# Turning keys and queries over in 64x64 quadrants in an attention and ReGLU kernel

## The chip, the cores and the metric

The kernel runs on one core of a Trainium2 chip. The metric is the device time of one execution in microseconds. The core has a matrix engine (TensorE, PE in the profile) that writes to PSUM, eight banks of 128 partitions by 512 fp32 values; three engines for elementwise work and reductions (VectorE or DVE, ScalarE or ACT, GpSimd or POOL); and DMA queues, of which this kernel uses that of SyncE (SP) for nearly everything and that of GpSimd for the weights of the feed-forward part.

## The reference

Eight batches of eight heads, 576 tokens, 64 values per head. Each head sees 16 "beacon" keys and values ahead of its own 576, the beacons from every row, the others causally. The heads are put side by side to 4608 tokens of 512 values, and a ReGLU feed-forward network follows.

```python
k_all = np.concatenate([beacon_k, k], axis=2)          # 16 + 576 = 592 keys
v_all = np.concatenate([beacon_v, v], axis=2)
scores = scale * np.matmul(q, k_all.transpose(0, 1, 3, 2))
scores = np.where(causal, -1000000000.0, scores)
a = np.exp(scores - scores.max(-1, keepdims=True))
a /= a.sum(-1, keepdims=True) + 1e-09
attn = np.matmul(a, v_all)
x = attn.transpose(0, 2, 1, 3).reshape(4608, 512)
out = (np.maximum(x @ w_gate, 0.0) * (x @ w_val)) @ w_out   # 512 -> 1536 -> 512
```

## The kernel before, in words

**Attention of one batch.** Heads are handled in four pairs, one head on partitions 0 to 63 and one on 64 to 127, so that a score matmul has 64 values to contract and TensorE can run four 64x64 quadrants side by side. Batch by batch, `new_batch` (line 497) loads the keys and queries of each pair (`load_pair`, 552), the last 64 keys with the beacons and the first and last queries (`load_rest`, 610) and the values (`load_v`, 647). A load lands as fp32 in one of eight staging buffers, is cast to bf16 into one of three cast buffers (`rounded`, 508; on GpSimd from batch 1 on) and is turned over so that the 64 values of a head lie on partitions.

In batches 0 to 6 that is done by TensorE: `turned` (522) issues four matmuls of 128x128 against an identity (line 529) into one PSUM bank, and ScalarE or VectorE evicts the bank to `kT` or `qT` (copies at 467 and 469). A load brings four neighbouring tokens (1 KB) to one partition, so the eviction puts columns back in order with a strided read. In batch 7 (`TURN`) a DMA transpose does it (574); its loads bring single tokens of 256 bytes (560).

**Scores to outputs.** `quad_scores` (727) computes a causal staircase of 64-query tiles for two pairs at a time, in the 64x64 shape (line 756). `softmax` (680) works along each row: minimum of negated scores and mask in one VectorE instruction (704), exponential with row sum on ScalarE (711), reciprocal on VectorE (717), normalisation in place on GpSimd (722). From batch 3 on a step takes two to four tiles. `last` (797) does the 16 last queries of all heads with 32-column tiles (806). `finish` (815) turns the probabilities over, by DMA except in batch 0 (and the last rows of batch 1), multiplies by the values (852, 875; shape 128x64 or 128x128) and copies to `xT`.

**Feed-forward.** `ffn` (905) takes ten spans of 240 to 512 tokens: gate (913) and value (918) matmuls, ReLU on ScalarE (924), product on VectorE (929), output matmuls (944), a copy and a store. A span waits for the batches that its tokens come from.

**What sets the order.** All of this is handed as tasks to a planner (`Plan`, 174) that simulates engines, buffers and DMA with costs written by hand and emits every engine's instructions in the order of that simulation. For each choice it takes the earliest possible start, then a term `late` for TensorE, then the priority. `late` belongs to the shape of the array: a task has a `part` (0: 128x128, 1: values, 2: scores, 3: last rows), a change costs SWITCH = 0.1, a task of the present part comes first, and a task with `lazy` of n may be put off up to n us while others run. Line 236:

```python
late = -1 if part and t.part == part else NEXT if part and t.part else \
    1 if part != t.part and at < t.ready + t.lazy else 0
```

BACKLOG limits how far loads and stores are issued ahead of the modelled wire. PACE x batch is the earliest planned start of a batch's scores. LAZY = 20 is the patience of the values. HELD and BEHIND hold single loads back: a tiny memset on GpSimd (539) must run before the load, and itself waits for a weight or, through BEHIND, for the normalised halves of an earlier batch. SC_MOST, V_MOST and F_MOST (5, 3, 3) limit how many PSUM banks scores, turns and values, and the feed-forward hold. Where TensorE has nothing planned before 160 us, filler matmuls (996) are put in.

Of the kernel before, what the change touches and what calls it, by code (L numbers as in the profile page):

```python
# [18 lines left out]

BACKLOG = 4.0  # L20
RANK1 = -14.0
AHEAD = 2.0
# [10 lines left out]
SLAZY = 0.0  # L33
NEXT = -0.5
ON_PE = 2
TURN = (7,)
TURN_FIRST = 100
# [27 lines left out]
AFTER = [[0.0, 12.0]]  # L65
PACE = 38.0

# [229 lines left out]
def kernel(  # L297
# [189 lines left out]


    def heads(src, b, s0, sl):
        return src[b, :, s0:s0 + sl, :].rearrange("h s d -> s h d")  # L490
# [6 lines left out]
    def new_batch(b, prio, work):  # L497
        t = Batch()
        t.b = b
        steps = 2 * sum(len(x) for x in (STEPS2 if b > BIGSTEP else STEPS if b >= SPLIT else STEPS_AB + STEPS_CDE)) + 1  # L500
        t.kT = Hold(kT_s, 2 * (NP + 1) + steps)
# [50 lines left out]
        def load_pair(kind, p, prio):  # L552

            src, s0 = {"k": (k, 0), "q": (q, 64 - Nb)}[kind]
            st = staged()

            def fetch(_):
                if b in TURN:
# [7 lines left out]
            ld = add("DMA", (1.0, TURN_LOAD) if b in TURN else (0.5, 0.87), fetch, (held,), (st,), prio[0])  # L566
            dst = t.kT if kind == "k" else t.q
            h16, ca = rounded(dst, st, P, neg_scale if kind == "q" else 1.0, prio, ld,
                              lambda to, src: [(to, src)] if b in TURN else [(
                to.rearrange("p (j h d) -> p h j d", h=2, j=4), src.rearrange("p (h j d) -> p h j d", h=2, j=4))])  # L570
            zeros = on_zeros.get(b) if kind == "q" else None
            c0 = Nb if kind == "k" else 64
            if b in TURN:
                t.rows[kind, p] = [add("DMA", (1.22, 0.177 * 4), lambda _: nc.sync.dma_start_transpose(
                    dst.tile[:, p, c0:c0 + MAIN].rearrange("p (j n) -> p j n", j=4), h16.tile), (ca, zeros), (h16, dst), prio[0] - TURN_FIRST)]
# [7 lines left out]
            t.rows[kind, p] = [add(("ACT", "DVE"), {"ACT": c_act(512), "DVE": c_dve(512)}, evict, (tu, zeros), (ps, dst), prio[1])]  # L583

        def load_half(kind, g, half, prio):
# [24 lines left out]
        def load_rest(kind, prio):  # L610
# [21 lines left out]
            def evict(x):  # L632
                ps3 = ps.tile.rearrange("p (a n) -> p a n", a=NP)
                if kind == "k":
                    copy(x.engine, dst.tile[:, :, Nb + MAIN:], ps3[:, :, :REST])
# [26 lines left out]

        at, held = 0, None
        for what in ORDER0 if b == 0 else "KQ0011v2233vvvv":
# [15 lines left out]
    def softmax(t, parts, ph, prio, k):  # L680
# [3 lines left out]
        def view(i, lo=0):  # L684
            n, held, off = parts[i][:3]
            if len(held) == 1:
                return held[0].tile[:, off + lo:off + n]
            at = 512 * next(j for j, x in enumerate(bank) if x is held[0].tile)
            return psum[:, at + lo:at + n]

# [6 lines left out]
        for i, (n, held, _, msk, m, on, _, scored) in enumerate(parts):  # L697
            first = []
            if m < n:
                first = [add("DVE", c_max(n - m), lambda _, i=i, n=n, m=m: nc.vector.tensor_reduce(  # L700
                    out=at(7), in_=view(i)[:, :n - m], axis=AX.X, op=ALU.min), (scored,), held, prio + 0.001 * i + 0.0005 * k, 0.25)]

            def lowest(_, i=i, n=n, m=m, msk=msk):
                nc.vector.tensor_tensor_reduce(out=view(i, n - m), in0=view(i, n - m), in1=msk, scale=1.0,  # L704
                                               scalar=at(7) if m < n else 3.0e38,
                                               op0=ALU.add, op1=ALU.min, accum_out=at(i))

            lows.append(add("DVE", c_max(m), lowest, (scored, on, *first), held, prio + 0.001 * i + 0.0005 * k, 0.25))
        for i, (n, held, _, _, _, _, a, _) in enumerate(parts):
            def exp(_, i=i, n=n, a=a):  # L710
                nc.scalar.activation(ph.tile.rearrange("p a n -> p (a n)")[:, a:a + n], view(i), AF.Exp,  # L711
                                     bias=at(i), scale=-1.0, accum_out=at(4 + i))
# [14 lines left out]
    def quad_scores(t, g, step, phs, vals, prio, after):  # L727
# [23 lines left out]
        def scores(_):  # L751
            for j, lo, n, b_, off in cols:
                for i in range(2):
                    for k in ks:
                        r = slice(64 * k, 64 * k + 64)
                        nc.tensor.matmul(banks[k][b_].tile[64 * i:64 * i + 64, off:off + n],  # L756
                                         t.q.tile[r, 2 * g + i, 64 * j:64 * j + 64],
                                         t.kT.tile[r, 2 * g + i, lo:lo + n], start=True, stop=True)

# [16 lines left out]
    def quad(t, g, vals, prio, after):  # L776
# [4 lines left out]
        if PEQ(t.b, g):  # L781
            todo = list(range(NB_AB)) if ab else [i for i in range(21) if i not in (3, 7)] if t.b < SPLIT else list(range(NB))
            on_pe = [todo[i:i + 8] for i in range(0, len(todo), 8)]
        phs = [Hold(Slots([p_ab[t.b][:, 2 * g + k]]) if ab else p_s[1], max(1, len(on_pe))) for k in range(2)]
# [12 lines left out]
    def last(t, prio):  # L797
# [5 lines left out]
        def scores(_):  # L803
            for bank, a, n in ((sc[0], 0, 512), (sc[1], 512, SK - 512)):
                for pp in range(NP):
                    nc.tensor.matmul(bank.tile[32 * pp:32 * pp + 32, :n], t.q.tile[:, pp, S + Nb - TAIL:],  # L806
                                     t.kT.tile[:, pp, a:a + n], start=True, stop=True)
# [7 lines left out]
    def finish(t, p, vals, ph, pt_s, blocks, on_pe, outs, prio):  # L815

        pt = Hold(pt_s, len(vals) + max(1, len(on_pe)))
        if on_pe:
            tr = []
            for todo in on_pe:  # L820
                tp = Hold(first_ps if t.b == 0 else v_ps, 2)
                z = len(todo)
                runs = []
                for i, a in enumerate(todo):
                    if not runs or runs[-1][1] + runs[-1][2] != a:
                        runs.append([i, a, 0])
                    runs[-1][2] += 1

                def turn(_, todo=todo, tp=tp):
                    to = tp.tile.bitcast(BF16)  # L830
                    for i, a in enumerate(todo):
                        nc.tensor.transpose(to[:, i * P:(i + 1) * P], ph.tile[:, a, :], ident)  # L832

                def evict(x, runs=runs, tp=tp):
                    for i, a, n in runs:
                        copy(x.engine, pt.tile[:, a:a + n, :].rearrange("p a n -> p (a n)"), tp.tile.bitcast(BF16)[:, i * P:(i + n) * P])

                u = add("PE", 0.06 * z, turn, outs + [on_ident], (ph, tp), prio - 4)
                more = 0.07 * (len(runs) - 1)
                tr.append(add(("ACT", "DVE"), {"ACT": c_act(z * P) + more, "DVE": 0.08 + 0.0006 * z * P + more}, evict, (u,), (tp, pt), prio - 4))  # L840
        else:
# [131 lines left out]
    for b in range(B):  # L973
        batches.append(new_batch(b, {0: -20, 1: RANK1}.get(b, b * T0 - 8), b * T0 - AHEAD if b else -20))
    for b in range(B):
        for i, vals in enumerate([("AB", "CDE")] if b >= SPLIT else [("AB",), ("CDE",)]):
            for g in range(2):
                quad(batches[b], g, vals, b * T0 + (4 * g if b >= SPLIT else 4 * i + 2 * g) - (AB_FIRST if b < SPLIT and i == 0 else 0), AFTER[b][i] if b < SPLIT else PACE * (b + g / 2))
        last(batches[b], b * T0 + 8)
    for t in batches:  # L980
# [49 lines left out]
```

## Time and profile before

| | us |
|---|---|
| median of 3 runs | 402.75 |
| the runs | 399.99, 402.75, 403.11 |
| the profiled execution | 399.48 |
| span of its instructions | 397.8 |
| TensorE busy | 386.6 |
| VectorE, ScalarE, GpSimd busy | 287.6, 261.7, 234.2 |

The profile is one execution. Its views: the page (busy time of each engine, the span in 40 slices), busy time in chosen stretches, groups of instructions by line with their count, mean duration and the idle time ahead of them, who waited for whom, the timeline, and the chain of waits, which follows the work that ended last back from releaser to releaser. Matmuls overlap, so one's duration (225 ns for 128 columns) is not what it costs in a row of others; that is read from starts, or from the chain. A line number can be that of a helper: 467 and 469 are all copies on ScalarE and VectorE.

### The profile page before, as it was taken

Reading aid. Unit: us, or ns where it says so; the run is one execution under the profiler, and the core shown is the slowest. Engines: PE = TensorE matmul, PEld = TensorE weight load, DVE = VectorE, ACT = ScalarE, POOL = GpSimd, SP = SyncE. Lnnn points to the kernel's source line nnn. Section 1 sums busy time; section 2 is a strip of 40 time slices with the busy share of each in tenths; the row PEclk is TensorE's granted clock in tenths of the full one; section 3 lists DMA queues with packets and bytes.
Section 4 is the critical chain, followed back from the end, with each engine's and each line's share of the span. In section 5 each row is a group of like instructions: output and inputs, shape, how many; then the busy total and the mean of one; then the engine's idle time right before and its main releaser. Section 6 shows DMA issues by size and latency. Waiting matters only on the chain.

```text
span 397.8 us, 9897 instructions
## 1 busy us (share of the span) xinstructions
PE 386.6 (97%) x3235; PEld 203.8 (51%) x3278; DVE 287.6 (72%) x1024; ACT 261.7 (66%) x820; POOL 234.2 (59%) x454
## 2 busy tenths in 40 slices
PE   6999999999999999999999999999999999999995
PEld 4667855655454545455455445444454544444543
DVE  3999899788988697879697969687758733342432
ACT  2999699868967788668877878587737721320320
POOL 6899979849977576869669848646653520000000
PEclk9999999999999999999999999999999999999999
DMA  7999989999999799989999989798979184001102
GB/s 183 233 205 226 250 154 180 214 232 256 247 209 204 197 224 221 176 227 263 189 166 298 208 146 183 164 221 184 196 138 234 25 127 145 2 0 57 50 1 93
DMA packets 184100, 68.87 MB, mean 173 GB/s; under 512 B 158384, under 2 KB 179504, under 8 KB 184048
## 3 DMA queue, kind: packets, MB, share of 16 engines
q1 hardware_dynamic: 179216, 63.46, 73.7%
q0 software_dynamic: 4752, 4.72, 7.5%
q8 instruction: 25, 0.41, 0.5%
q14 instruction: 27, 0.22, 0.2%
q10 hardware_dynamic: 80, 0.07, 0.1%
HBM read 38.54 MB, written 9.44 MB: 121 GB/s over the span
## 4 chain that ended last, share of the span: by engine, by line
PE 88%; POOL 3%; DVE 3%; DMA 2%; issue 1%; SPq 1%; ACT 0%; POOLq 0%; ACTq 0%
PE f L918 23%; PE f L944 23%; PE f L913 22%; PE f L756 7%; PE f L852 6%; PE f L529 3%; DMA st<-in_q_dram 2%; POOL xT L722 2%; DVE f L704 2%; PE f L832 1%; PE f L996 1%; PE f L875 1%; PE f L806 1%; DVE osb L469 1%; POOL h L518 1%
## 5 line engine op out<-in xcount | busy, mean ns | idle before, releaser
L722 POOL TENSOR_SCALAR pb<-pb,small 128x448 bf16<-128x448 bf16 (+8 forms) x272 | 141.5, 539 | 70.5 <-DVE small L717 69.8
L711 ACT ACTIVATE pb<-f,small 128x320 bf16<-128x320 f32 (+8 forms) x272 | 143.9, 553 | 22.6 <-DVE small L704 17.7
L704 DVE CUSTOM_DVE_ANT_0 f<-f,mask 128x576 f32<-128x576 f32 (+8 forms) x288 | 133.7, 515 | 14.3 <-PE f L756 9.1
L918 PE MATMUL f<-xT,wv_r 128*128 128x512 bf16 (+3 forms) x467 | 107.3, 358 | 0.7
L913 PE MATMUL f<-xT,wg_r 128*128 128x512 bf16 (+3 forms) x468 | 105.4, 357 | 0.6
L929 DVE TENSOR_TENSOR hT<-g,f 128x512 bf16<-128x512 f32 (+3 forms) x120 | 75.4, 631 | 37.3 <-PE f L918 32.1
L944 PE MATMUL f<-wo_r,hT 128*128 128x512 bf16 (+3 forms) x438 | 99.6, 374 | 1.3 <-issue 0.5
L924 ACT ACTIVATE g<-f 128x512 f32<-128x512 f32 (+3 forms) x120 | 66.3, 562 | 50.9 <-PE f L913 44.2
L913 PEld LDWEIGHTS <-wg_r 128*128 128x128 bf16 x480 | 45.3, 98 | 43.7 <-issue 1.2
L918 PEld LDWEIGHTS <-wv_r 128*128 128x128 bf16 x480 | 43.4, 98 | 44.5 <-issue 5.2
L944 PEld LDWEIGHTS <-hT 128*128 128x128 bf16 (+2 forms) x456 | 42.1, 100 | 46.3 <-issue 2.1
L711 ACT ACTIVATION_READ_ACCUMULATOR pb<-f,small 128x1 f32 x272 | 60.9, 224 | 0.0
L518 POOL TENSOR_SCALAR h<-st 128x512 bf16<-128x512 f32 (+1 forms) x93 | 49.0, 541 | 11.0 <-DMA st<-in_q_dram 6.9
L469 DVE COPY osb<-f 128x512 f32<-128x512 f32 (+2 forms) x32 | 21.7, 682 | 28.1 <-PE f L944 27.7
L704 DVE DVE_READ_ACCUMULATOR2_ANT small<- 128x1 f32 x296 | 41.6, 141 | 0.0
L467 ACT CAST xT<-f 128x240 bf16<-128x240 f32 (+2 forms) x56 | 21.2, 385 | 30.7 <-PE f L852 29.5
L756 PE MATMUL f<-kT,qT 64*64 64x512 bf16 (+7 forms) x640 | 34.4, 295 | 0.1
L717 DVE RECIPROCAL small<-small 128x1 f32<-128x1 f32 (+3 forms) x136 | 20.9, 161 | 13.5 <-ACT pb L711 9.8
L529 PE MATMUL f<-ident,h 128*128 128x128 bf16 (+1 forms) x288 | 26.8, 222 | 1.6 <-POOL h L518 1.4
L529 PEld LDWEIGHTS <-h 128*128 128x128 bf16 (+1 forms) x288 | 20.0, 101 | 14.6 <-POOL h L518 4.0
L852 PE MATMUL f<-pTb,v 128*64 128x320 bf16 (+3 forms) x488 | 26.7, 253 | 0.0
L471 POOL TENSOR_SCALAR v<-st 128x512 bf16<-128x512 f32 (+1 forms) x38 | 23.2, 617 | 4.0 <-DMA st<-in_v_dram 4.0
(61 smaller groups left out, 217.5 us busy)
## 6 DMA issues: line engine op xcount, KB each, us to landing
out_dram<-osb SPq DMA_DIRECT2D x34, 256.0 KB, 2.4
st<-in_k_dram SPq DMA_DIRECT2D x28, 256.0 KB, 5.0
st<-in_q_dram SPq DMA_DIRECT2D x28, 256.0 KB, 5.1
st<-in_v_dram SPq DMA_DIRECT2D x24, 256.0 KB, 5.6
st<-in_k_dram SPq DMA_DIRECT2D x16, 128.0 KB, 4.2
st<-in_q_dram SPq DMA_DIRECT2D x16, 128.0 KB, 3.1
st<-in_v_dram SPq DMA_DIRECT2D x8, 224.0 KB, 5.2
wg_r<-in_moe_w_gate_dram POOLq DMA_DIRECT2D x3, 512.0 KB, 7.3
```

The lines of the kernel that those rows point to most:

```text
L518: (nc.gpsimd if x.engine == "POOL" else nc.vector).tensor_scalar(to, src, by, 1.0, ALU.mult, ALU.mult)
L529: nc.tensor.matmul(to, h16.tile[:rows, a * P:(a + 1) * P], ident[:rows, :rows], start=True, stop=True)
L704: nc.vector.tensor_tensor_reduce(out=view(i, n - m), in0=view(i, n - m), in1=msk, scale=1.0, scalar=at(7) if m < n else 3.0e38, op0=ALU.ad ...
L711: nc.scalar.activation(ph.tile.rearrange("p a n -> p (a n)")[:, a:a + n], view(i), AF.Exp, bias=at(i), scale=-1.0, accum_out=at(4 + i))
L722: nc.gpsimd.tensor_scalar(one, one, at(8 + i), 1.0, ALU.mult, ALU.mult)
L756: nc.tensor.matmul(banks[k][b_].tile[64 * i:64 * i + 64, off:off + n], t.q.tile[r, 2 * g + i, 64 * j:64 * j + 64], t.kT.tile[r, 2 * g + i, ...
L852: nc.tensor.matmul(ps.tile[64 * hh:64 * hh + 64, d0:d0 + w], t.v.tile[:rows, c, D * h:D * h + D], rhs(64 * hh), start=(c == 0), stop=(c == ...
L913: nc.tensor.matmul(psg.tile[:, :mt], wg_r[:, ki, nf * P:(nf + 1) * P], xT[:, ki, m0:m0 + mt], start=(ki == 0), stop=(ki == KM - 1))
L918: nc.tensor.matmul(psv.tile[:, :mt], wv_r[:, ki, nf * P:(nf + 1) * P], xT[:, ki, m0:m0 + mt], start=(ki == 0), stop=(ki == KM - 1))
L924: r = add("ACT", c_act(mt), lambda _, psg=psg, g=g: nc.scalar.activation(g.tile[:, :mt], psg.tile[:, :mt], AF.Relu), (a,), (psg, g), -1000 ...
L929: hid.append(add("DVE", c_dve(mt), lambda _, psv=psv, g=g, nf=nf: nc.vector.tensor_mul(hT[nf].tile[:, :mt], g.tile[:, :mt], psv.tile[:, :m ...
L944: nc.tensor.matmul(ps[c].tile[64 * c:64 * c + rows, :w], hT[nf].tile[:, t0:t0 + rows], wo_r[:, nf, w * c:w * c + w], start=(nf == 0), stop ...
```

## The change

Four things are changed. **Quadrants**: in batches 4 to 6 the turns of a pair's keys and queries wait for each other (`waiting`) and become one task, `turned_pair`, of 32 matmuls of 64x64 with `part=2`, the shape of the scores, and with a laziness of 4 us plus LAZIES of the batch. Its result lies in two neighbouring banks, one for each half of the partitions, and two evictions read both. The cost given to the planner is 0.24. **Batch 7's keys**: still turned by DMA, but loaded like the others in 1-KB runs. The transposed keys then lie in four runs (every fourth key), with 12 columns of padding ahead of each; scores, mask, exponential and the evictions of the rest go through strided views, so the probabilities come out in order. **Order**: BACKLOG, NEXT, PACE and BEHIND get other values, and loads, scores, ranks, last rows and laziness get one number per batch. **Unused code**: the same quadrants for probabilities, off by PQUADS = 0.

```diff
-BACKLOG = 4.0
+BACKLOG = 6.0
-NEXT = -0.5
+NEXT = 0
-TURN = (7,)
+QUADS = 4
+TLAZY = 4.0
+KTURN = (7,)
+QTURN = (7,)
+PQUADS = 0
-BEHIND = {(2, 2): (1, 0), (2, 7): (1, 1)}
+BEHIND = {(2, 7): (1, 0)}
-PACE = 38.0
+PACE = 36.0
+LOADS = [0, 0, 0, 0, 0, 0, 0, 0]
+STEPS_AT = [0, -6, 0, 0, -3, 6, 0, 0]
+RANKS = [0, 0, 0, 0, 0, 0, 0, 6]
+LASTS = [8, 8, 8, 0, 8, 0, 8, 12]
+LAZIES = [0, 0, 4, 0, 0, 0, 8, 8]
...
+    RUN = 4
+    KW, KPAD = SK // RUN, 12
-    kT_s = Slots(many(2, [P, NP, SK], BF16, "kT"))
+    kT_s = Slots(many(2, [P, NP, RUN * (KPAD + KW)], BF16, "kT"))
...
+    def by_run(x):
+        return x.rearrange("p (j m) -> p j m", j=RUN)
+    def key_runs(x):
+        return by_run(x)[:, :, KPAD:]
+    def in_order(x):
+        return x.rearrange("p (m j) -> p j m", j=RUN)
...
+            if b >= QUADS:
+                t.rows[kind, p] = []
+                waiting.append((kind, dst, h16, ca, zeros, p))
+                if len(waiting) == 2:
+                    turned_pair(prio)
                 return
...
+        def turned_pair(prio):
+            todo, waiting[:] = list(waiting), []
+            ps = [Hold(v_ps, 3) for _ in range(2)]
+            ps[0].next, ps[1].prev = ps[1], ps[0]
+            def turn(_):
+                for x, (_, _, h16, _, _, _) in enumerate(todo):
+                    for j in range(4):
+                        for r in range(2):
+                            for c in range(2):
+                                rows = slice(64 * r, 64 * r + 64)
+                                nc.tensor.matmul(ps[r].tile[64 * c:64 * c + 64, 256 * x + 64 * j:256 * x + 64 * j + 64],
+                                                 h16.tile[rows, j * P + 64 * c:j * P + 64 * c + 64], ident[rows, rows],
+                                                 start=True, stop=True)
+            tu = add("PE", 0.24, turn, [x[3] for x in todo] + [on_ident], (*[x[2] for x in todo], *ps), prio[1],
+                     part=2, lazy=TLAZY + LAZIES[b])
...
+                    both = psum[:, at:at + 1024].rearrange("p (r y) -> p r y", r=2)[:, :, 256 * x:256 * x + 256]
+                    copy(e.engine, dst.tile[:, p, c0:c0 + MAIN].rearrange("p (r n j) -> p r n j", r=2, j=4),
+                         both.rearrange("p r (j n) -> p r n j", j=4))
...
+                if t.runs:
+                    own, against = by_run(own) if m == n else view(i)[:, :, 512 // RUN:], in_order(msk)
...
+                if t.runs:
+                    to, x = in_order(to), by_run(x) if whole[i][0] != SK else x
...
+                            keys = [(off, n, runs[:, :, :w])] if j < TILES else [(0, 3 * w, runs[:, :3, :w]), (3 * w, 512 - 3 * w, runs[:, 3, :512 - 3 * w])] if lo == 0 else [
+                                (off, n, runs[:, 3, w - n:w])]
...
-        batches.append(new_batch(b, {0: -20, 1: RANK1}.get(b, b * T0 - 8), b * T0 - AHEAD if b else -20))
+        batches.append(new_batch(b, {0: -20, 1: RANK1}.get(b, b * T0 - 8 + LOADS[b]), b * T0 - AHEAD if b else -20))
```

In the same way STEPS_AT is added to the planned start of a batch's scores, RANKS to their priority, and LASTS takes the place of 8 in that of the last rows. SK is 592, RUN is 4: a run is 148 keys.

More of the change, by code (lines that the diff above doesn't have):

```diff
@@ L661, in load_v @@
                                  (ld,), (st, t.v), prio[1])
-        at, held = 0, None
+        at, held, waiting = 0, None, []
         for what in ORDER0 if b == 0 else "KQ0011v2233vvvv":
@@ L827, in finish, with turn_quads @@
                     runs[-1][2] += 1
+                def turn_quads(_, todo=todo, tps=tps):
+                    for i, a in enumerate(todo):
+                        for k in range(2):
+                            for c in range(2):
+                                rows, cols = slice(64 * k, 64 * k + 64), slice(64 * c, 64 * c + 64)
+                                nc.tensor.transpose(tps[k].tile.bitcast(BF16)[cols, i * 64:i * 64 + 64], ph.tile[rows, a, cols], ident[rows, rows])
                 def turn(_, todo=todo, tp=tp):
@@ L977 @@
             for g in range(2):
-                quad(batches[b], g, vals, b * T0 + (4 * g if b >= SPLIT else 4 * i + 2 * g) - (AB_FIRST if b < SPLIT and i == 0 else 0), AFTER[b][i] if b < SPLIT else PACE * (b + g / 2))
-        last(batches[b], b * T0 + 8)
+                quad(batches[b], g, vals, b * T0 + RANKS[b] + (4 * g if b >= SPLIT else 4 * i + 2 * g) - (AB_FIRST if b < SPLIT and i == 0 else 0), AFTER[b][i] if b < SPLIT else PACE * (b + g / 2) + STEPS_AT[b])
+        last(batches[b], b * T0 + LASTS[b])
     for t in batches:
```

72 lines of the change are left out of this document (52 added, 20 removed).

## The prediction

> **What bounds the kernel now.** I read the page first, then busy time by stage, the waits of TensorE, the groups by line, and last the chain of waits and short stretches around the steps that the change touches.
>
> ```profile
> PE 386.6 (97%) x3235; PEld 203.8 (51%) x3278; DVE 287.6 (72%) x1024; ACT 261.7 (66%) x820; POOL 234.2 (59%) x454
> PE   6999999999999999999999999999999999999995
> ```
> ```profile
> 0.00:50.00 50.00, 45.88 (x544) 33.40 (x544) 39.97 (x190) 37.97 (x116) 43.45 (x89) 1.00 1.11 219
> ...
> 140.00:310.00 170.00, 168.14 (x1391) 82.34 (x1415) 136.11 (x475) 127.76 (x414) 114.13 (x218) 1.00 0.96 200
> ```
> ```profile
> PE f L996 <- POOL mask L415: 2.0, 1, 2.0
> PE f L529 <- POOL h L518: 1.4, 3, 0.8
> PE f L832 <- POOL xT L722: 0.6, 1, 0.6
> PE f L944 <- issue: 0.5, 3, 0.2
> ```
>
> TensorE is the bound. It is busy nine tenths or more of every slice but the first and the last; from 140 to 310 us it works 168.14 of 170 us, and in the whole run it waits 4.5 us for others (2.0 + 1.4 + 0.6 + 0.5). The granted clock in these stages is 1.00, so no throttle is in it. The time is what TensorE has to issue, plus gaps inside "busy" that come from changing the shape of the array. An edit that takes work off VectorE, ScalarE or the DMAs alone buys nothing; one that takes a matmul or a change of shape off TensorE buys its length. What does TensorE do besides the FFN? In the whole run, and then in the first 50 us:
>
> ```profile
> L529 PE MATMUL f<-ident,h 128*128 128x128 bf16 x224 | 21.4, 225 | 1.5 <-POOL h L518 1.4
> ```
> ```profile
> L996 PE MATMUL f<-mask,ident 128*128 128x256 bf16 x87 | 15.5, 307 | 2.0 <-POOL mask L415 2.0
> ```
> ```profile
> PEld L756 <- issue: 17.4, 48, 0.4
> ```
> ```profile
> 156.28 0.45 PE f L529 x8
> 156.73 0.86 PE f L913 x4
> 157.59 0.22 PE f L529 x4
> 157.81 0.56 PE f L756 x16
> 158.38 0.97 PE f L918 x4
> 159.35 1.73 PE f L913 x8
> ```
>
> The last fence, of the chain, holds the prices. FFN matmuls of 512 columns go at 1.73/8 = 0.216 us. Turning over one pair of heads (L529, four matmuls) takes 0.22 us, two take 0.45, with no gap towards the FFN, since the shape is the same. A visit to the 64x64 shape for scores (L756) takes 0.56 us; its 1024 columns per quadrant would take 0.43 at the FFN's pace, 0.13 less, and the four FFN matmuls behind it take 0.97 instead of 0.86, 0.11 more. So a visit costs 0.24 us above its columns. The weight loads say the same: at 48 of the visits they first stand idle, 17.4/48 = 0.36 us each.
>
> **The quadrants.** Batches 4 to 6 (counted from 0) have 24 of the 224/4 = 56 turns: 24 x 0.22 = 5.3 us of TensorE, all on the path. They become 12 couples, keys and queries of one pair of heads. A couple is 32 matmuls of 64x64 with 64 columns, that is eight groups of four which fill the four quadrants. What is a group worth? The trace has one group of 64 columns in the middle of a visit:
>
> ```profile
> 131.92:131.93 0.01, 0.01 (x5) 0.00 (x1) 1.00 1.44 282
> 131.93:131.94 0.01, 0.01 (x8) 0.01 (x4) 1.00 1.02 179
> 131.94:131.95 0.01, 0.01 (x8) 0.01 (x4) 1.00 0.74 128
> 131.95:131.96 0.01, 0.01 (x10) 0.01 (x4) 1.00 2.12 333
> 131.96:131.97 0.01, 0.01 (x12) 0.01 (x4) 1.00 1.06 179
> ```
>
> These are stretches of 10 ns, L756 alone; the first x counts matmuls in flight, the second weight loads. The 64-column group enters around 131.93 (5, then 8 in flight), and the next, whose weight loads began with it, around 131.96: 30 ns a group. Eight make 0.24 us, against 0.45 before. Two other groups of 64 columns are slower, each the first of its visit:
>
> ```profile
> 137.37:137.38 0.01, 0.01 (x3) 0.01 (x3) 1.00 0.29 102
> ...
> 137.42:137.43 0.01, 0.01 (x6) 0.01 (x9) 1.00 1.31 307
> 137.43:137.44 0.01, 0.01 (x8) 0.01 (x12) 1.00 0.00 0
> ```
> ```profile
> 11.56:11.58 0.02, 0.02 (x4) 0.02 (x4) 1.00 0.96 230
> ...
> 11.64:11.66 0.02, 0.02 (x7) 0.02 (x7) 1.00 1.07 256
> ...
> 11.72:11.74 0.02, 0.02 (x11) 0.02 (x8) 1.00 1.32 333
> ```
>
> At 137.37 the second group follows after 0.055 us, at 11.56 after 0.08, and there the third after 0.08 again: eight groups would take 0.44 or 0.64. I take 0.24, the value of the group whose loads could run ahead, as seven of a couple's eight can; the ends stay for the range. A couple by itself pays the visit too: 0.24 + 0.24 = 0.48 for 0.45, a loss of 0.03. One that joins a score visit wins 0.45 - 0.24 = 0.21. How many join? A turn may wait for company (TLAZY and LAZIES add up to 4, 4 and 12 us in the three batches).
>
> ```profile
> 177.23 0.63 PE L756 MATMUL f<-kT,qT 64*64 64x64 bf16 x16
> ...
> 184.42 0.63 PE L756 MATMUL f<-kT,qT 64*64 64x192 bf16 x12
> ```
>
> Score visits are 7.2 us apart here, with batch 5's turns between and beside them. A couple takes two neighbouring PSUM banks of the three that V_MOST allows, so hardly more than one fits a visit; and while it waits it keeps two of the three cast buffers, so the next cast stands behind it on GpSimd's queue, and the normalisations behind that. I reckon 4/7.2 of eight and three of the last four, 7 of 12: 7 x 0.21 - 5 x 0.03 = 1.3 us off. All twelve would give 2.5; none, at 0.64, 12 x (0.64 + 0.24 - 0.45) = 5.2 us more.
>
> [...]
>
> Evictions keep their elements (twice 128x512 per couple, each from two banks now). A strided read of PSUM is what they had before, too:
>
> ```profile
> L469 DVE CAST kT<-f 128x512 bf16<-128x512 f32 x15 | 10.2, 682 | 1.8 <-PE f L529 1.8
> L469 DVE COPY osb<-f 128x512 f32<-128x512 f32 x30 | 20.6, 690 | 27.3 <-PE f L944 27.0
> ```
>
> It takes 682 ns strided, 690 straight. I take no difference; were it double, 24 x 0.68 = 16 us of VectorE would lie in a stage where it works 136.11 of 170.
>
> **Batch 7's keys** are turned by DMA before and after, so TensorE gains nothing. Their loads go from two issues to one per pair of heads, from 256-byte to 1-KB runs, so SP's queue is spared four issues, for which TensorE doesn't wait (its waits above name none on a load). In exchange the batch's 36 softmax parts run through strided views (mask reads on VectorE 16 bytes apart, bf16 writes on ScalarE 8 bytes apart), the scores take four runs as one operand, and the last rows' scores are 16 matmuls over 576 columns for 8 over 592. The trace shows no strided SBUF access on these engines, so each part costs between nothing and as much again.
>
> ```profile
> L711 ACT ACTIVATE pb<-f,small 128x64 bf16<-128x64 f32 (+8 forms) x18 | 9.4, 536 | 1.6 <-DVE small L704 1.5
> ```
> ```profile
> 319.08 2.37 POOL L722 TENSOR_SCALAR pb<-pb,small 128x576 bf16<-128x576 bf16 x4 [3.57 <-DVE small L717]
> ```
> ```profile
> 333.63 1.50 PE f L852 x32
> ```
>
> The first row is of the stretch from 298 to 336 us. As much again is 36 x 0.54 = 19 us of ScalarE. The cover is this: batch 7's normalisation ends at 321.45 and its values run at 333.63, with the FFN that needs them right behind: 12 us. The new PACE lets the batch begin 14 us earlier (2 us for each batch before it), 26 us in all. I take zero on the path. [...]
>
> **Order and pace.** BACKLOG lets loads be issued 2 us further ahead, so a transpose of probabilities may stand 2 us longer behind them in SP's queue; values may wait 20 us for company anyway, which covers it. Of batch 2's two held loads one goes free and the other waits for an earlier half. NEXT, RANKS, STEPS_AT and LASTS reorder. What that is worth no row tells; its stock is 15.5 us of fillers, 0.24 us a visit and 4.5 us of waits. I take zero and keep 3 us (a fifth of the fillers, or twelve visits) to both sides.
>
> **The sum** is -1.3 us. The profiled execution took 399.48 us (span 397.8 and 1.7 around it), 3.3 under the median of 402.75; the runs were 399.99, 402.75 and 403.11. Two executions lie near 400 and two near 403, mean 401.3. Less 1.3, that is 400.0.
>
> **Rivals.** (a) *The order wins too.* All couples join (2.5) and batches 2 us closer together fill 3 us of filler time: 401.3 - 5.5 = 395.8. For it: 15.5 us of fillers. Against: they lie in the first 50 us, where the DMA share is 1.11 already and no couple is. (b) *The quadrants go at the pace of issue*, as at 11.56: slower. It decides where a couple is let go by a cast that has only just ended, so that no instructions stand ready behind it; break-even is 0.45/8 = 0.056 us a group. At 0.08 and five visits more: 12 x 0.19 + 5 x 0.24 = 3.5 more, 404.8. [...] (c) *Couples hold buffers*: casts and normalisations stand behind two kept buffers, batch 7 starts no earlier, its parts double, and TensorE, with only its rows left at 335 us, stands for 19 - 12 = 7 us: 408. Against: GpSimd works 114.13 of 170. (d) *A wash*: groups are bound by weight loads at 0.055, or nothing joins: 401.3 to 402.4.
>
> **Numbers.** Forecast 0.44, (a) 0.21, (b) 0.10, (c) 0.12, (d) 0.13. One per cent is about what a measurement of this kernel can tell from no change: 398.7 and 406.8. The forecast's own range is 397 to 403 (3 us of order both ways), a third of it below 398.7: 0.15. Of (a) 0.18 is below, so faster 0.33. Slower is a quarter of (b), most of (c) and some scatter: 0.03 + 0.10 + 0.01 = 0.14. The rest is 0.53. A range that leaves out 2 in 10 goes from (a) to between (b) and (c): 395.3 to 406.
>
> **What would show it.** Right: 64x64 matmuls at the new turning line beside scores, about 0.24 us a couple in the chain; L529's 128x128 matmuls down from 224 to 128; no more visits than before; waits of TensorE still under 5 us. Wrong: groups at 0.055 us or more; couples between two FFN stretches; TensorE waiting for GpSimd's casts between 140 and 240 us; a gap ahead of 335 us; fillers under 12 us, which is (a).

## The result and the profile after

| | before | after |
|---|---|---|
| median | 400.25 us | 412.68 us |
| the runs | 399.49 to 403.11 (6) | 410.37 to 417.65 (6) |
| the profiled execution | 399.48 us | 410.37 us |
| span of its instructions | 397.8 us | 408.7 us |

The ratio is 1.029, with an interval of 1.021 to 1.036: slower. (Ratios here and below leave disturbed executions out, the medians do not, so they can differ a little from the quotient of the medians.) The two spans differ by 10.9 us.

The page of after: busy time, then TensorE and its granted clock in 40 slices of 10.2 us.

```profile
PE 392.9 (96%) x3583; PEld 204.5 (50%) x3583; DVE 289.0 (71%) x1019; ACT 277.3 (68%) x831; POOL 233.7 (57%) x453
...
PE   6999999999999999999999999999779899999995
...
PEclk9999999999999999999999999999998899999999
```

Before, every slice of TensorE between the first and the last was a 9. Now three are not (two of them from 286 to 306 us, one from 317 to 327), and the clock falls in two slices, from 306 to 327. The slices ahead of that are as full as they were; the loss lies in one place. Beside TensorE itself, ScalarE alone has much more busy time, 277.3 - 261.7 = 15.6 us. Who is TensorE waiting for? The waits of after, TensorE's alone (waiting line, releaser: us in total, times, longest):

```profile
PE f L832 <- ACT pb L780: 3.6, 4, 1.7
...
PE f L1005 <- ACT pa L780: 1.0, 1, 1.0
PE f L1010 <- ACT pb L780: 0.8, 1, 0.8
...
PE f L944 <- ACT pb L780: 0.5, 1, 0.5
```

L780 is the exponential (711 before). In the profile of before no wait of TensorE on it was among the larger ones; here it is 3.6 + 1.0 + 0.8 + 0.5 = 5.9 us. The timeline of TensorE in after shows where (start, us, line, tiles, what; in brackets the idle time ahead and its releaser):

```profile
280.70 0.64 PE L832 MATMUL f<-kT,qT 64*64 64x64 bf16 x16
...
284.68 2.75 PE L1036 MATMUL f<-wo_r,hT 128*128 128x512 bf16 x12
...
288.92 0.71 PE L944 MATMUL f<-pTb,v 128*64 128x320 bf16 x10 [0.55 <-ACT pb L780]
...
295.22 0.33 PE L832 MATMUL f<-kT,qT 64*64 64x64 bf16 x7 [1.66 <-ACT pb L780]
...
305.62 3.31 PE L1005 MATMUL f<-xT,wg_r 128*128 128x512 bf16 x8 [0.96 <-ACT pa L780]
...
322.99 0.48 PE L832 MATMUL f<-kT,qT 64*64 64x64 bf16 x7 [1.34 <-ACT pb L780]
323.40 2.88 PE L944 MATMUL f<-pTb,v 128*64 128x128 bf16 x32
...
328.53 1.89 PE L1005 MATMUL f<-xT,wg_r 128*128 128x512 bf16 x8
...
343.30 1.57 PE L944 MATMUL f<-pTb,v 128*64 128x128 bf16 x32
```

The scores of batch 7 begin at 280.70; the values of its two halves run at 323.40 and 343.30. The waits are in the middle of the batch, not at its end: TensorE is about to write scores (or, in three of the seven waits, values or a product of the FFN) into a PSUM bank that ScalarE hasn't read yet, and everything behind in its fixed order stands too. The row at 305.62 shows a second loss. Eight FFN matmuls take 3.31 us there and 1.89 at 328.53. Short stretches of after say why (us, then busy time of PE, PEld, DVE, ACT, POOL with counts, granted clock, DMA share, GB/s):

```profile
304.00:305.00 1.00, 0.48 (x12) 0.23 (x7) 0.75 (x2) 1.00 (x3) 1.00 (x2) 1.00 0.00 0
305.00:306.00 1.00, 0.38 (x2) 0.19 (x2) 0.40 (x2) 0.56 (x2) 1.00 (x3) 0.96 0.07 16
306.00:307.00 1.00, 1.00 (x3) 0.29 (x2) 1.00 (x6) 0.00 (x0) 1.00 (x3) 0.50 0.00 0
...
323.00:324.00 1.00, 1.00 (x17) 0.69 (x18) 0.56 (x2) 0.87 (x3) 0.76 (x2) 0.50 0.00 0
```

Ahead of each fall TensorE was idle for more than half of two microseconds (busy 0.86 us from 304 to 306, 0.44 from 321 to 323); then the clock is halved for 3.4 us: from 305.9 to 309.3, and again from 323.0 to 326.4. Adding (1 - clock) over the stretches of 1 us gives 1.7 us lost in each, 3.4 together. So here the idle time is followed by a bill of its own, 3.4 us.

And why is ScalarE late? The parts of batch 7 that are 576 wide, after (groups by line and shape, from 280 to 335 us: count, busy us, mean ns, idle time ahead):

```profile
L780 ACT ACTIVATE pb<-f,small 128x576 bf16<-128x576 f32 x4 | 5.8, 1544 | 1.6 <-POOL v L482 1.6
...
L770 DVE CUSTOM_DVE_ANT_1 f<-f,mask 128x576 f32<-128x576 f32 x4 | 4.6, 1208 | 0.4 <-PE f L832 0.4
```

The same shapes of all batches, before:

```profile
L711 ACT ACTIVATE pb<-f,small 128x576 bf16<-128x576 f32 x32 | 23.7, 744 | 6.6 <-DVE small L704 6.4 <-DVE small L717 0.2
...
L704 DVE CUSTOM_DVE_ANT_0 f<-f,mask 128x576 f32<-128x576 f32 x32 | 23.9, 773 | 5.3 <-PE f L756 2.6 <-POOL pb L722 2.5
```

An exponential written 8 bytes apart takes 1544 ns for 744, twice as long; a minimum whose mask is read 16 bytes apart takes 1208 for 773.

The quadrants themselves did what they should. A visit with a couple, and one without, on the timeline of TensorE in after:

```profile
142.22 0.63 PE L832 MATMUL f<-kT,qT 64*64 64x192 bf16 x12
142.67 0.42 PE L624 MATMUL f<-ident,h 64*64 64x64 bf16 x32
143.03 1.90 PE L1010 MATMUL f<-xT,wv_r 128*128 128x512 bf16 x8
...
160.11 0.63 PE L832 MATMUL f<-kT,qT 64*64 64x192 bf16 x12
160.67 1.90 PE L1010 MATMUL f<-xT,wv_r 128*128 128x512 bf16 x8
```

From the scores to the FFN it is 0.81 us with a couple (142.22 to 143.03) and 0.56 without (160.11 to 160.67): 0.25 us a couple, 31 ns for a group of four. Ten of the twelve couples stand beside scores like this one.

### The profile page after: what moved, and what is told of

Same layout as the page of the kernel before. It is cut to its first block, busy times and chain, and to the rows that moved or that the text cites. A ratio compares the mean times of both kernels' runs of the same rounds, so it can differ in the third digit from the quotient of the medians.

```text
span 408.7 us, 10560 instructions
## 1 busy us (share of the span) xinstructions
PE 392.9 (96%) x3583; PEld 204.5 (50%) x3583; DVE 289.0 (71%) x1019; ACT 277.3 (68%) x831; POOL 233.7 (57%) x453
## 4 chain that ended last, share of the span: by engine, by line
PE 81%; ACT 6%; DVE 3%; DMA 3%; POOL 2%; issue 2%; SPq 1%; ACTq 0%; DVEq 0%; POOLq 0%
PE f L1010 23%; PE f L1005 23%; PE f L1036 19%; PE f L944 5%; PE f L832 5%; ACT pb L780 4%; DMA st<-in_v_dram 3%; PE f L550 2%; DVE f L770 2%; POOL pb L791 2%; PE f L919 1%; PE f L967 1%; PE f L624 1%; SPq L675 1%; PE f L882 1%
## 5 line engine op out<-in xcount | busy, mean ns | idle before, releaser
L791 POOL TENSOR_SCALAR pb<-pb,small 128x320 bf16<-128x320 bf16 (+8 forms) x272 | 141.6, 538 | 81.6 <-DVE small L786 80.9
L780 ACT ACTIVATE pb<-f,small 128x320 bf16<-128x320 f32 (+8 forms) x272 | 156.5, 614 | 24.7 <-DVE small L770 15.5
L770 DVE CUSTOM_DVE_ANT_0 f<-f,mask 128x64 f32<-128x64 f32 (+8 forms) x252 | 117.6, 512 | 13.0 <-PE f L832 9.2
L1036 PE MATMUL f<-wo_r,hT 128*128 128x512 bf16 (+2 forms) x456 | 102.6, 374 | 0.0
L780 ACT ACTIVATION_READ_ACCUMULATOR pb<-f,small 128x1 f32 x272 | 63.4, 233 | 0.0
L832 PE MATMUL f<-kT,qT 64*64 64x64 bf16 (+8 forms) x648 | 35.7, 292 | 4.3 <-ACT pb L780 3.6
L480 DVE COPY osb<-f 128x512 f32<-128x512 f32 (+2 forms) x26 | 17.6, 679 | 23.6 <-PE f L1036 23.5
L478 ACT CAST xT<-f 128x240 bf16<-128x240 f32 (+2 forms) x44 | 17.0, 391 | 24.9 <-PE f L944 23.6
L944 PE MATMUL f<-pTb,v 128*64 128x320 bf16 (+3 forms) x488 | 29.2, 262 | 1.0 <-ACT pb L780 0.5
L832 PEld LDWEIGHTS <-qT 64*64 64x64 bf16 x648 | 14.7, 106 | 28.7 <-issue 24.6
L944 PEld LDWEIGHTS <-v 128*64 128x64 bf16 (+1 forms) x512 | 22.2, 113 | 9.7 <-issue 6.0
```

Of the source, the lines that this page charges most:

```text
L770: nc.vector.tensor_tensor_reduce(out=own, in0=own, in1=against, scale=1.0, scalar=at(7) if m < n else 3.0e38, op0=ALU.add, op1=ALU.min, ac ...
L780: nc.scalar.activation(to, x, AF.Exp, bias=at(i), scale=-1.0, accum_out=at(4 + i))
L791: nc.gpsimd.tensor_scalar(one, one, at(8 + i), 1.0, ALU.mult, ALU.mult)
L832: nc.tensor.matmul(banks[k][b_].tile[64 * i:64 * i + 64, at:at + w], t.q.tile[r, 2 * g + i, 64 * j:64 * j + 64], x, start=True, stop=True)
L944: nc.tensor.matmul(ps.tile[64 * hh:64 * hh + 64, d0:d0 + w], t.v.tile[:rows, c, D * h:D * h + D], rhs(64 * hh), start=(c == 0), stop=(c == ...
L1036: nc.tensor.matmul(ps[c].tile[64 * c:64 * c + rows, :w], hT[nf].tile[:, t0:t0 + rows], wo_r[:, nf, w * c:w * c + w], start=(nf == 0), stop ...
```

## The experiments

The theory at this point: the exponentials of batch 7, twice as long, let banks go late (A). Rivals: the mask reads on VectorE do it (B); it is the quadrants or the order, and batch 7 only shows it (C). "Straight" below means that a view runs in the order in which the data lie in memory, with the same number of elements.

### Which strided access

**The batch as it was.** Loads of 256-byte runs and straight views for batch 7, all else as after.

```diff
-        t.runs = b in KTURN
+        t.runs = False
...
-                if kind == 'q' and b in QTURN:
+                if b in QTURN:
...
```

> The changed kernel with batch 7's keys loaded and laid out as before (256-byte runs, no strided views); quadrants and all order values stay. Theory S (the strided views of batch 7's softmax double the exponentials, and TensorE stands in its fixed order between 285 and 330 us): the loss goes, 397 to 401 us, 128x576 exponentials at 0.74 us throughout, waits of TensorE under 5 us. Rival O (the new order values cost the time): 408 to 413. Rival Q (quadrants cost it): 408 to 413.

Measured: 414.38 us, ratio 1.037 (1.029 to 1.045). The waits on the exponential are gone, but another is there: TensorE's values (L944) wait 11.3 us, once 9.1 at a stretch, for the transposed probabilities of batch 7 (`pTb`). So this is no clean undoing: with the other parts of the change in place, the old batch 7 is late in a way that it wasn't before. It is taken up again below.

**Straight writes.** The loads stay, and only the exponentials' destination changes, so the probabilities of batch 7 stand in the wrong columns.

```diff
-                    to, x = in_order(to), by_run(x) if whole[i][0] != SK else x
+                    x = by_run(x) if whole[i][0] != SK else x
+                    to = by_run(to)
```

> The changed kernel, batch 7's exponentials written straight, in the order of the runs (so batch 7's probabilities stand in the wrong columns); the mask is still read 16 bytes apart. Every engine's order is that of the changed kernel. If the strided writes of ScalarE carry the loss: 128x576 exponentials back from 1.54 to about 0.75 us and 400 to 404 us. If VectorE's strided mask reads (1.21 for 0.77 us) carry it: 407 to 411.

Measured: 403.64 us, ratio 1.005 (0.9998 to 1.010). The profiled execution has a span of 399.7 us for after's 408.7. Groups by line and shape of this kernel:

```profile
L781 ACT ACTIVATE pb<-f,small 128x576 bf16<-128x576 f32 x32 | 23.9, 750 | 9.6 <-DVE small L770 8.5 <-POOL pb L792 0.9
...
L770 DVE CUSTOM_DVE_ANT_1 f<-f,mask 128x576 f32<-128x576 f32 x4 | 4.7, 1212 | 0.6 <-PE f L833 0.6
```

The exponentials of all batches take 750 ns again, and the mask reads are as slow as in after. Its order on TensorE is that of after, so the two timelines can be laid side by side. This kernel's, for the first and last row shown of after:

```profile
285.93 2.75 PE L1037 MATMUL f<-wo_r,hT 128*128 128x512 bf16 x12
...
319.57 1.89 PE L1006 MATMUL f<-xT,wg_r 128*128 128x512 bf16 x8
```

The same instructions take 33.64 us here and 43.85 in after (284.68 to 328.53): 10.2 us. Of these, 5.9 are the waits on the exponential, 0.4 other idle time (two waits for `hT`, 0.6 together there and 0.2 here), and 3.4 the halved clock: 9.7. The other 0.5 us is not accounted for.

**Straight mask**, and **both straight**:

```diff
-                    own, against = by_run(own) if m == n else view(i)[:, :, 512 // RUN:], in_order(msk)
+                    own, against = by_run(own) if m == n else view(i)[:, :, 512 // RUN:], by_run(msk)
```

> The changed kernel, the mask of batch 7 read straight (so batch 7 masks wrong columns); the exponentials are still written 8 bytes apart. Order as in the changed kernel. If ScalarE's writes carry the loss: minimum steps of 128x576 back to 0.77 us and still 407 to 411 us. If VectorE's reads carry it: 400 to 404.

> The changed kernel with both straight (batch 7's mask and probabilities in the wrong columns), key runs, score operands and 1-KB loads kept. Theory S: all of the loss goes, 397 to 402 us. Rival (the four-run score operands, the evictions into runs, or the order): 407 or more.

Measured: with the mask alone 412.19 us, 1.024 (1.012 to 1.036), hardly off after's; with both 403.96, 1.003 (0.998 to 1.009), by these intervals no better than the writes alone. In the first, VectorE's 576-wide minima are back at 773 ns and the exponential is as in after:

```profile
L770 DVE CUSTOM_DVE_ANT_0 f<-f,mask 128x576 f32<-128x576 f32 x32 | 23.9, 773 | 4.5 <-POOL pb L791 2.7 <-PE f L832 1.7
...
L780 ACT ACTIVATE pb<-f,small 128x576 bf16<-128x576 f32 x32 | 26.6, 846 | 8.1 <-DVE small L770 7.0 <-POOL pb L791 0.9
```

(28 at about 746 and 4 at 1544 make a mean of 846.) So B falls as the main cause: as long as ScalarE is slow, VectorE's extra time is covered. It isn't quite free once ScalarE is fast: with both straight, the stretch that takes 33.64 us with the writes alone takes 32.36 (290.92 to 323.28 in its profile), 1.3 us less, without any idle time of TensorE; the fastest executions, 398.85 and 400.17 us, differ by as much.

### What the strides cost by themselves

In the kernel before, the exponentials of batches 4, 5 and 6 are written 4, 8 and 16 bytes apart (`j` = 2, 4, 8), and the mask of batch 7 is read 8 bytes apart.

```diff
+                j = {4: 2, 5: 4, 6: 8}.get(t.b, 1)
+                if j > 1:
+                    to, x = to.rearrange("p (m j) -> p j m", j=j), x.rearrange("p (j m) -> p j m", j=j)
...
+                if t.b == 7:
+                    own, against = own.rearrange("p (j m) -> p j m", j=2), against.rearrange("p (m j) -> p j m", j=2)
```

> Prices of strided access, measured in the kernel before: the exponentials of batch 4 are written 4 bytes apart, of batch 5 8 bytes, of batch 6 16 bytes (their probabilities stand in the wrong columns), and batch 7's mask is read 8 bytes apart (wrong columns masked). If every write that isn't next to the last costs one more slot: 128x576 exponentials at 1.5 us in all three batches. [...]

Groups by line and shape: straight, then 4, 8 and 16 bytes on ScalarE, then 8 bytes on VectorE.

```profile
L725 ACT ACTIVATE pb<-f,small 128x576 bf16<-128x576 f32 x20 | 14.9, 749 | 1.9 <-DVE small L707 1.7 <-DVE small L730 0.2
...
L719 ACT ACTIVATE pb<-f,small 128x576 bf16<-128x576 f32 x4 | 3.5, 903 | 1.7 <-DVE small L707 1.7
...
L721 ACT ACTIVATE pb<-f,small 128x576 bf16<-128x576 f32 x4 | 6.0, 1544 | 1.7 <-DVE small L707 1.7
...
L723 ACT ACTIVATE pb<-f,small 128x576 bf16<-128x576 f32 x4 | 11.0, 2876 | 0.7 <-DVE small L707 0.7
...
L707 DVE CUSTOM_DVE_ANT_1 f<-f,mask 128x576 f32<-128x576 f32 x4 | 3.0, 773 | 0.8 <-PE f L769 0.7
```

749, 903, 1544 and 2876 ns: writing bf16 every 4 bytes costs a fifth, every 8 bytes twice the time, every 16 almost four times. From 8 to 16 bytes it grows by 1332 ns over 576 elements, 2.3 ns each. VectorE's fp32 reads 8 bytes apart cost nothing (773), 16 apart half as much again (1208 in after). The kernel as a whole took 439.43 us.

### The other parts alone

Rival C: the quadrants alone, the order alone, and batch 7's edit alone. In the first two, batch 7 is the old one, by the edit shown first.

The quadrants alone, by the order of before:

```diff
-BACKLOG = 6.0
+BACKLOG = 4.0
-NEXT = 0
+NEXT = -0.5
-BEHIND = {(2, 7): (1, 0)}
+BEHIND = {(2, 2): (1, 0), (2, 7): (1, 1)}
-PACE = 36.0
+PACE = 38.0
-STEPS_AT = [0, -6, 0, 0, -3, 6, 0, 0]
-RANKS = [0, 0, 0, 0, 0, 0, 0, 6]
-LASTS = [8, 8, 8, 0, 8, 0, 8, 12]
+STEPS_AT = [0] * 8
+RANKS = [0] * 8
+LASTS = [8] * 8
```

The order alone, by `QUADS = 8`, which no batch reaches. Batch 7 alone, by both of these edits, with its new loads and views.

> The kernel before with the quadrants of batches 4 to 6 alone: order values and batch 7 as before. Theory S (the quadrants win what was forecast, about 0.2 us a joined couple): 397 to 400 us. Rival Q (quadrants disturb the order or hold buffers): 403 or more. Rival F (any change of the plan late in the run moves batch 7's end and TensorE starves there): a wait of TensorE of several us before the last two spans, 404 or more.

> The kernel before with the new order values alone (no quadrants, batch 7 as before). Theory S: within 2 us of before, 398 to 403. Rival O (the new values put batch 7's second half too late unless its keys come in 1-KB runs): TensorE waits 5 to 12 us for the transposed probabilities of batch 7, 406 to 414.

> The kernel before with batch 7's keys in 1-KB runs and the strided views alone (no quadrants, order values as before). Theory S: 128x576 exponentials of 1.54 us in batch 7 and TensorE waiting for ScalarE there, 406 to 412. Rival (c of the prediction: the batch's cover of 12 us absorbs its slower parts): 398 to 403.

| | median | ratio |
|---|---|---|
| quadrants alone | 413.28 us | 1.031 (1.026 to 1.035) |
| order alone | 413.83 us | 1.031 (1.027 to 1.034) |
| batch 7 alone | 410.18 us | 1.022 (1.017 to 1.027) |

Each part alone is slower than before. Batch 7 alone has after's fault, in its waits of TensorE:

```profile
PE f L832 <- ACT pb L780: 3.5, 5, 1.5
```

With 1.1, 0.7 and 0.7 us on other lines this makes 6.0 us of waits on the exponential, for 5.9 in after.

The other two have the one seen in the first experiment: values that wait for transposed probabilities, 9.5 us with the order alone, 9.4 with the quadrants alone. The longest of the latter, on the timeline of TensorE:

```profile
339.50 1.55 PE L944 MATMUL f<-pTb,v 128*64 128x128 bf16 x16 [6.30 <-DMA pTb<-pb]
```

Why are they late? The timeline of SP's queue in that kernel:

```profile
287.60 1.06 SPq L581 DMA_DIRECT2D st<-in_q_dram  x2
...
295.76 3.83 SPq L934 DMA_TRANSPOSE pTb<-pb  x1
...
300.80 4.38 SPq L934 DMA_TRANSPOSE pTb<-pb  x1
305.23 1.26 SPq L597 DMA_TRANSPOSE qT<-h  x1
```

and in the kernel before:

```profile
275.10 1.05 SPq L560 DMA_DIRECT2D st<-in_q_dram  x2
...
293.61 1.21 SPq L574 DMA_TRANSPOSE qT<-h  x1
294.94 3.76 SPq L842 DMA_TRANSPOSE pTb<-pb  x1
...
299.92 4.27 SPq L842 DMA_TRANSPOSE pTb<-pb  x1
```

The last queries of batch 7 are loaded 12.5 us later (287.60 for 275.10) and turned over behind two transposes of probabilities, which hold the queue for 4 us each, instead of ahead of them: 305.23 for 293.61. They are cast to bf16 (on GpSimd) only 2.8 us later, at 293.36 for 290.55, so most of the 11.6 us is the place behind the two transposes. After has them at 291.4; with the order alone, in a profile with 4.3 us of another wait ahead, they come at 314.0, behind two transposes as well. So it is an order of SP's queue that comes out differently, not a price of the quadrants, and with the new loads of batch 7 it doesn't come out so.

### Telling the planner, and another way to the same layout

**The true cost.** The planner is told what the strided parts take (for VectorE somewhat more: 1.65 times, where 1208 for 773 ns is 1.56).

```diff
-            lows.append(add("DVE", c_max(m), lowest, (scored, on, *first), held, prio + 0.001 * i + 0.0005 * k, 0.25))
+            lows.append(add("DVE", c_max(m) * (1.65 if t.runs else 1), lowest, (scored, on, *first), held, prio + 0.001 * i + 0.0005 * k, 0.25))
-            sums.append(add("ACT", c_exp(n), exp, [lows[i]] + same + on_pads + on_ab_pads, held, prio + 0.001 * i + 0.0005 * k, 0.25))
+            sums.append(add("ACT", c_exp(n) + (0.0014 * n if t.runs else 0), exp, [lows[i]] + same + on_pads + on_ab_pads, held, prio + 0.001 * i + 0.0005 * k, 0.25))
```

> The changed kernel whose planner is told the measured cost of batch 7's parts (ScalarE 1.4 ns more per element, VectorE's steps 1.65 times as long); the instructions are the same, their order is planned anew. If the loss is TensorE standing in a fixed order that expected results sooner: 399 to 405, waits of TensorE on ScalarE near zero. If the strided work itself is too much for the stage: 407 or more.

Measured: 424.69 us, 1.060 (1.056 to 1.064), the slowest of the variants of the change. The waits on the exponential are gone, as the theory had it, but TensorE waits longer than anywhere else for transposed probabilities:

```profile
PE f L944 <- DMA pTb<-pb: 16.1, 2, 13.9
```

This is not the late load again: the last queries are turned at 294.98. The probabilities themselves are late: those of the batch's second half are turned at 344.48, where after has them at 332.39. Why the planned order came out like this is open, so the run decides neither for the theory nor for its rival.

**The keys reordered once.** The 1-KB loads stay, the DMA transpose goes to a buffer of its own, and one copy for each pair of heads on ScalarE or VectorE puts the keys in order; the 36 parts are straight again. First with the quadrants in before's order, then the same without quadrants (`QUADS = 8`), and then with all of the change, its order too (and a second such buffer).

```diff
-        t.runs = b in KTURN
+        t.runs = False
...
+                kr = Hold(kr_s, 2)
+                tr = add("DMA", (1.22, 0.177 * 4), lambda _: nc.sync.dma_start_transpose(kr.tile, h16.tile), (ca,), (h16, kr), prio[0] - TURN_FIRST)
...
+                def natural(x):
+                    copy(x.engine, dst.tile[:, p, c0:c0 + MAIN].rearrange("p (n j) -> p n j", j=RUN), kr.tile.rearrange("p j n -> p n j"))
...
```

> The quadrants with the order values of before, as in the run with the quadrants alone, but batch 7's keys in 1-KB runs: the DMA transpose writes the four runs to a small buffer and one copy per pair of heads on ScalarE or VectorE puts them in order, so no softmax part is strided. Theory L (the run with the quadrants alone was slow because batch 7's last keys and queries were loaded too late, not for the quadrants): 397 to 400 us, no wait of TensorE for transposed probabilities. Rival Q (the quadrants themselves cost): 408 or more.

> The kernel before with batch 7's keys in 1-KB runs, put in order by one copy per pair, and nothing else (no quadrants, order values of before). Theory L: within 1.5 us of before (399 to 402), as there was no late load to cure; the difference from the run before this one is then the quadrants alone, about 1.5 to 2.5 us. Rival (1-KB runs are worth time by themselves): 398 or less.

> All of the change, order values too, with batch 7's keys put in order by one copy per pair instead of 36 strided softmax parts. Theory: the strided exponentials were the loss, so 396 to 400 us. Rival (the new order values cost by themselves, as the run of the changed kernel with old loads for batch 7 might be read): 404 or more.

| | median | ratio |
|---|---|---|
| quadrants, keys copied | 400.99 us | 1.003 (0.999 to 1.006) |
| no quadrants, keys copied | 402.89 us | 1.005 (1.002 to 1.007) |
| all of the change, keys copied | 402.37 us | 0.999 (0.995 to 1.003) |

Four copies, in the first of these (tile `kR`: when each was, shape):

```profile
L483 DVE COPY kT<-kR x3: 599/600/608, 264.5 to 283.5; 128x512 bf16<-128x512 bf16 x3
L481 ACT COPY kT<-kR x1: 1094/1094/1094, 293.2 to 293.2; 128x512 bf16<-128x512 bf16 x1
```

3 x 0.60 + 1.09 = 2.9 us of engine time do the work for which ScalarE's exponentials took 12.6 us more in after (`pb`, all batches: 156.5 for 143.9), and the last queries of batch 7 are in time, on the timeline of SP's queue of the same kernel:

```profile
290.48 1.73 SPq L609 DMA_TRANSPOSE qT<-h  x1
...
301.52 3.92 SPq L946 DMA_TRANSPOSE pTb<-pb  x1
```

Between this kernel and the quadrants alone, which is 1.031, only the way of batch 7's keys differs. Whether its fewer issues, its longer runs or the lower cost that the planner has for them brings the queries forward is not shown.

All three medians lie 0.9 to 2.4 us above what was expected, and no version beats the kernel before by more than the measurement can tell. The medians with and without quadrants differ by 402.89 - 400.99 = 1.9 us, which is the size that the couples give (below). But the intervals of the two ratios overlap, and the fastest execution of both is 399.56 us: the quadrants' worth is not shown by the times.

## Why the prediction was wrong, point by point

**The bound.** TensorE is the bound, as read, outside batch 7; in the first 280 us it is busy for 275.07 us in after and 273.49 in before. (Of the 4.5 us of waits, 0.5 are marked "issue", a wait for nothing that the profile shows.)

**The quadrants.** Right, and better than taken. 0.24 us a couple was forecast, 0.25 is measured; 128x128 turns went from 224 to 128 as forecast; ten couples join a visit where seven were taken. By the prediction's own prices that is 10 x 0.21 - 2 x 0.03 = 2.0 us off, for 1.3. The groups in after:

```profile
L550 PE MATMUL f<-ident,h 128*128 128x128 bf16 x128 | 11.8, 225 | 1.4 <-POOL h L539 1.2
...
L624 PE MATMUL f<-ident,h 64*64 64x64 bf16 x384 | 5.3, 193 | 0.0
```

**The evictions.** No difference was taken; VectorE's 128x512 to `kT` takes 688 ns after and 682 before.

**Batch 7: the step that failed.** The prediction bounded each part "between nothing and as much again" and put 19 us of ScalarE at the upper end. For the widest parts the upper end is what came, 1544 for 744 ns; ScalarE is busy 15.6 us longer in all. (Besides the 36 parts, the exponential of the last rows is written with strides too, 1609 ns for 764. Their scores still run over 592 keys, in 16 matmuls of 148 columns, not over 576.) The failure is the next step, "I take zero on the path", and the cover of 26 us that it came from. Little of that cover was there.

The 12 us between the normalisation and the values of the kernel before were not free. The values wait for two transposes of the probabilities, on SP's queue in before:

```profile
320.31 8.39 SPq L842 DMA_TRANSPOSE pTb<-pb  x2
```

The second is issued at 324.9 and lands about 6 us later (5.7 and 6.5 us for the two), so that some 2.5 us are left before 333.56. The 14 us from PACE didn't come either. The batch's first scores are at 280.70 in after, and in before at

```profile
275.49 0.63 PE L756 MATMUL f<-kT,qT 64*64 64x64 bf16 x16
```

which is 5.2 us earlier: PACE is an earliest start for the planner, not a start. And the end of the batch was the wrong place to look. In between, each exponential has to free a bank of scores for the next visit of TensorE, whose order is written down beforehand: the scores stood 1.66 us at 295.22 and 1.34 at 322.99, while the values of these halves run only at 323.40 and 343.30. That the strided exponentials do it the straight writes show (10.2 us of the stretch gone with one view changed). The work on `L711` alone was no way to see this; the row to ask for is who writes next to the bank that an exponential reads, and how long after.

**Order and pace, ±3 us.** Wrong as a bound. In one surrounding the order is worth nothing that can be measured (all of the change with copied keys 0.999, without the new order 1.003); with batch 7's old loads it is 1.031, 12.8 us, and there the last queries stand behind two transposes in SP's queue. The prediction's stock, fillers and visits, didn't have SP's queue in it, and the 1-KB loads were read as sparing "four issues, for which TensorE doesn't wait". With them, in every version that has them, the last queries come in time.

**The rivals.** (c) came nearest: its 408 has the doubled parts and a TensorE that stands. It also has that batch 7 starts no earlier, which is so (5.2 us later). The rest of its way there, kept buffers and one stop of 7 us at 335, is not what happened; the stops lie from 288 to 323, and a third of the price (3.4 of 10.2 us) is the clock. (a) fell in so far as the order wins nothing in any version; (b)'s pace of 0.08 us a group, 0.64 a couple, is in none of the twelve, which take 0.42 to 0.45 from the first start to the last end; (d), a wash, is in size what the change is with its strided writes taken out, though not for (d)'s reasons: couples join, at 31 ns a group.

**The clock.** "No throttle is in it" was true of the kernel before, whose clock is 1.00 in every microsecond up to 396, where TensorE has ended, and not of the changed one, where it is 0.50 for 3.4 us twice while TensorE works. Read in stretches of 0.1 us, the falls and rises lie on a grid: the two falls, at 305.92 and 322.99, are five times 3.41 us apart, and each rise, at 309.33 and 326.40, comes 3.41 us after its fall. The kernel with exponentials at three strides has the same grid between 290 and 335 us: by its clock in stretches of 1 us it falls at 290.5, 300.8 and 314.4, three and four times 3.41 apart, and stays halved for 3.4, 6.8 and 3.4 us. So in these stretches of the two traces the clock changes only at such times.

What sets a fall off is not shown. It was no single long wait: in the 3.41 us before the first, TensorE was busy for 1.84, and no wait was over 0.96 us. Nor is it the busy time alone, as the grid's window from 292.27 to 295.68 holds only 1.75 us of work and no fall follows it. With batch 7 alone, whose waits are as long (6.0 us for 5.9), the clock stays at 1.00 from 250 to 350 us. A prediction that has TensorE stand for some microseconds should allow for the clock: in after it is 3.4 us on 6.3 of added idle time, with batch 7 alone nothing in this stage.

## What to carry to other kernels

Price a change of layout at every consumer: 36 strided writes cost 12.6 us of an engine, four copies ahead of them 2.9. A gap between two rows is slack only if nothing that the second needs runs in it, on a DMA queue for instance (of the 12 us before, two transposes left some 2.5). And slack at the end of a stage says nothing of its middle: where TensorE runs in a fixed order over a few banks, an engine that reads those banks is on the path as soon as it ends later than TensorE's next use of the bank (1.66 us at 295.22, with the values of that half at 323.40). Lastly, a part that is harmless in one order of the queues can cost 3% in another (the quadrants: 1.003 and 1.031), so that parts are to be tried together with what sets the order, and alone, before one of them is called the cause.

## What was not expected of the hardware

ScalarE's bf16 writes are dearer by stride than VectorE's fp32 reads: for 128x576, 749, 903, 1544 and 2876 ns at 2, 4, 8 and 16 bytes apart, against 773, 773 and 1208 for the reads at 4, 8 and 16.

A wait of TensorE for a copy to `xT`, between 22 and 26 us, is no fixed part of a planned order: with straight writes alone it is 0.7 us in the profile (span 399.7 us), with both views straight, in the same order, 4.5 (403.4 us). What sets it is open.
